# Two plain MLP groups instead of four, and five Strassen pairs instead of four, with each later Fourier mix set beside the next batch's attention

## The chip, the cores and the metric

The kernel runs on one core of one Trainium2 chip. The metric is the device time of one execution in microseconds (us). The core has five engines with a queue each: TensorE (PE in the profile, its weight loads PEld), VectorE (DVE), ScalarE (ACT), GpSimd (POOL) and SyncE (SP). Each works through its queue in order; semaphores make one wait for another. DMA transfers are issued from the queues of SP, ACT and POOL. Everything is float32, and each float32 matmul has two records in the trace (a transpose has one).

## The reference

```python
# attention: q, k, v (4, 8, 768, 64), lam (8,); blocks of 64 along the sequence
intra = (qb @ kb.T * Dmask) @ vb                  # Dmask[i, j] = lam ** (i - j) for i >= j
inter = (qb * lam_pow) @ kv_state
out = intra + inter
kv_state = lam_block * kv_state + (kb * rev_pow).T @ vb
x = out.transpose(0, 2, 1, 3).reshape(4, 768, 512)
# mix and MLP: w_ch1 (512, 2048), w_ch2 (2048, 512)
mixed = real(fft(fft(x, axis=1), axis=2))
u = x + mixed
un = (u - mean(u)) / sqrt(var(u) + 1e-6)          # over the last axis
return u + maximum(un @ w_ch1, 0) @ w_ch2
```

## The kernel before

**The front.** For each of the four batches, `attn(b)` computes the attention in six chunks of 128 rows, and `fft_ln(b)` the Fourier mix and the normalisation. One chunk: transposes of k and q (L314, L319), scores (L338, TensorE), scores times decay (L343, VectorE), the state (L358 on TensorE, L363 on VectorE), old state times q (L373), scores times v (L379), a turn back (L395), and copies by ACT. `kd`, the decayed k (L310), is made by POOL. x goes to DRAM, and POOL's queue gathers its mirrored rows (L489, L495 after chunk 4, L502 after the last chunk). The mix uses symmetry: VectorE folds x with its mirror (`fold_a`, `fold_b` or `folds_apart`, tiles `fe` and `fo`, L476 to L571), TensorE transforms along the sequence (L603, twenty products a batch), ACT copies to `ys`, TensorE transforms along the width (`width`, L615 to L620), and VectorE adds the result to x (`summed`, L691 to L704), three times. Then `stats` (L634, L635, with POOL's L638 and L639 for `rs`) and `norm` (L655) follow for three groups of 256 rows each, numbered 1, 2, 0.

**The MLP** of the twelve groups is done in two ways. A *plain* group is `mlp(b, g)`: `norm` transposes on TensorE (L660) and keeps `ut` in SBUF; the first layer is 64 products of 128x128x256 (L749), with the maximum on ACT (L757) or VectorE (L755), the second 32 products of 128x128x512 (L763). It can run beside the front. A *late* group goes to DRAM instead, transposed by VectorE (L668, four stores of 64 KB a tile on SP's queue), with its u (256 KB a tile). After the front, two late groups make a *pair*, done in Strassen's form: the first pair with one level in the first layer (L1031) and two in the second (L1198), the later, *deep* pairs with two levels in both (L1124 and L1198, 392 products of 128x128x128 each way). Two lines say which groups are which:

```python
    ORDER = [(b, g) for b in range(B) for g in (1, 2, 0)]
    PLAIN, LATE = ORDER[:4], ORDER[4:]
```

Strassen's form needs sums of weight quarters. `combine_weights(0)` and `(1)` (L837, sixteen VectorE operations, tiles `w1s`, `w2s` and, in place, the weights `w`) come after the front; their space is that of the front's tables. `front_sums` (L265) makes some more in the front and stores them by POOL's queue. `late()` then runs the pairs; the first pair starts with `begin`, six sets of products with plain weights, and the next product needs `w1s` and `sx` (L929, L931).

**The order.** What sets it is Python generators that yield an estimate of their time: `weave(lead, other, ratio)` takes steps of `other` whenever its sum lags behind that of `lead`, `beside` is a weave with a part of another generator, `chain` runs one after the other. Operations are emitted in that order, a scheduler may move them somewhat (`keep_in_program_order` and `high_priority` steer it), and then each engine's order is fixed. Before, the rest of the front is one chain, with each batch's attention and then its mix, and the plain groups lie along all of it:

```python
    fr = chain([att1, fft_ln(1)] + [front(b) for b in range(2, B)])
    run(beside(beside(chain(half[0]), t_half, w, 0.5 * NW), t_half + 0.5 * NW, fr, t_rest * t_half / t_back + 15.0))
    run(w)
    back = chain(half[1] + [mlp(*PLAIN[3])])
    run(weave(fr, back, (t_back - t_half) / (t_rest - t_rest * t_half / t_back)))
```

Three of the four plain groups are split into two halves of the hidden layer, since half of the weights arrive first (`w`, the generator that loads the weights and brings them to the form used, L226 to L235); what is left of the last plain group is emitted with `combine_weights(0)`. Batch 0's mix has run beside attention 1 already (`LEADS`), before the plain groups.

Of the kernel before, what the change touches and what calls it, by code (L numbers as in the profile page):

```python
# [77 lines left out]
def kernel(  # L78
# [11 lines left out]
    B, H, S, D = q.shape  # L90
# [38 lines left out]
    xp = plain_pool("xp", 2 * NC + 2)  # L129
    up = plain_pool("up", 3)  # L130
# [198 lines left out]
    def attn_out(b, c, head):  # L329
# [75 lines left out]
        if b not in TURNED:  # L405
# [9 lines left out]
            if (b, c) == (B - 1, 1):  # L415
                with tc.issue_after(grown.ins):
                    run(front_sums())
# [160 lines left out]
    def fft_ln(b):  # L578
# [7 lines left out]
        if b in LEADS:  # L586
            yield from fold_a(b)
            yield from fold_b(b, sets)
            yield 2.0
        else:  # L590
            yield 1.0
            run(fold_a(b))
            yield 6.0 if b - 1 in LEADS else 3.0
            run((folds_apart if b > 1 else fold_b)(b, sets))
            yield 27.0 if b - 1 in LEADS else 9.0
# [46 lines left out]
        def norm(g):  # L642
# [7 lines left out]
            for i in range(G):  # L650
                un = new(ep, [128, DM], "e") if i == 1 and (b, g) in (PLAIN[0], PLAIN[3]) else new(np_, [128, DM], "un", bufs=1)
                u = xs[b, TT[g][i]]
                with tc.high_priority(300) if (b, g) in PLAIN[1:3] else ExitStack():
                    for o, x in ((un[:, 0:HM], u[:, 0:HM]), (un[:, HM:DM], u[:, DM - 1:HM - 1:-1])):
                        nc.vector.tensor_scalar(o, x, mv[:, i, 0:1], rs[:, i:i + 1],  # L655
                                                op0=ALU.subtract, op1=ALU.mult)
# [63 lines left out]
        if b in LEADS:  # L720
            two, none = norm(2), norm(0)
            held.update({(b, 1, 1): two, (b, 1, 4): two, (b, 1, 7): none, (b, 1, FO): none})
            return
# [5 lines left out]
    PLAIN, LATE = ORDER[:4], ORDER[4:]  # L729
# [624 lines left out]
    def run(gen):  # L1354
        return sum(gen)
# [28 lines left out]
    half = [[mlp(b, g, h * FO // 2, (h + 1) * FO // 2) for b, g in PLAIN[:3]] for h in range(2)]  # L1384
    half[0][0] = mlp(*PLAIN[0], 0, FO // 2, half[0][1])
    fr = chain([att1, fft_ln(1)] + [front(b) for b in range(2, B)])
    t_rest, t_back = 3 * t_front - 5 * t_chunk, len(PLAIN) * t_mlp - 50.0
    t_half = 1.5 * t_mlp
    run(beside(beside(chain(half[0]), t_half, w, 0.5 * NW), t_half + 0.5 * NW, fr, t_rest * t_half / t_back + 15.0))
    run(w)  # L1390
    back = chain(half[1] + [mlp(*PLAIN[3])])
    run(weave(fr, back, (t_back - t_half) / (t_rest - t_rest * t_half / t_back)))
# [45 lines left out]
```

## Time and profile before

| | |
|---|---|
| three runs | 777.11, 777.5 and 780.93 us; median 777.5 us |
| span of the profiled execution | 771.7 us; its own time is not listed apart, 5.8 us lie between its span and the median |
| attention 0, mix 0 and most of attention 1 | 0 to 94.7 us |
| plain groups beside the front | from 94.7 us on |
| scores of batch 3's last chunk | 333.3 us |
| first product of the first Strassen pair | 409.6 us |
| first products of the three deep pairs | 501.4, 588.9 and 676.5 us |

The span is from the first to the last instruction on the core. A row of a table by stretches gives the length, then for each engine the busy time and in brackets its instructions, then the granted TensorE clock, the DMA share and the GB/s. A row of the timeline gives start, duration, engine, line, operation, tiles (out<-in), shape and count, and in brackets how long the engine had been idle and what ended that. Lines are those of the kernel before; in the changed kernel most of these stand three lines higher (L749 is L746 there).

### The profile page before, as it was taken

To read this page: it belongs to the slowest core of one execution; us is meant where nothing else is said; L and a number is where in the kernel's file an instruction comes from. 1 tells how busy PE (TensorE), PEld (TensorE's weight loads), DVE (VectorE), ACT (ScalarE), POOL (GpSimd) and SP (SyncE) were. 2 spreads that over 40 slices of the span, in tenths; PEclk is the share of its full clock that TensorE was granted. 3 is DMA by queue.
4 is the path that set the end of the run, shared out by engine and by line. 5 is a ranking of instruction groups with operands and counts; after the bars stand their busy time and mean duration, and the time that the engine had idled before them with its cause. 6 is when DMAs were issued, how large, how long until landed. Compare 5 with 4: busy or idle time off the path is not lost.

```text
span 771.7 us, 15006 instructions
## 1 busy us (share of the span) xinstructions
PE 752.6 (98%) x5784; PEld 646.7 (84%) x5784; DVE 602.8 (78%) x1167; ACT 231.1 (30%) x532; POOL 178.4 (23%) x202
## 2 busy tenths in 40 slices
PE   6989999999999999999999999999999999999997
PEld 5777877777685967769747899999999999999997
DVE  6999998784936575336898999788986699758984
ACT  3755443435521221322101221034301341024310
POOL 3223330021111113220105941360015001230013
PEclk9999999999999999999999999999999999999999
DMA  9979732347943149731433465876545456455442
GB/s 240 274 161 250 195 125 86 106 96 181 246 117 94 45 82 270 176 97 35 113 65 124 150 218 164 273 234 202 180 124 178 125 186 182 127 175 180 144 141 70
DMA packets 154924, 120.22 MB, mean 156 GB/s; under 512 B 114286, under 2 KB 116974, under 8 KB 154854
## 3 DMA queue, kind: packets, MB, share of 16 engines
q1 hardware_dynamic: 147792, 100.51, 46.7%
q0 software_dynamic: 4032, 12.99, 4.7%
q10 hardware_dynamic: 3030, 5.78, 2.1%
q8 instruction: 46, 0.75, 0.4%
q14 instruction: 24, 0.20, 0.1%
HBM read 88.04 MB, written 31.20 MB: 155 GB/s over the span
## 4 chain that ended last, share of the span: by engine, by line
PE 88%; DVE 7%; DMA 2%; ACT 1%; issue 1%; POOL 0%; SPq 0%; DVEq 0%; ACTq 0%
PE p L1198 22%; PE p L1124 17%; PE pm L763 13%; PE pm L749 13%; PE p L1031 6%; PE pa L603 3%; PE pa L379 3%; PE pa L338 3%; PE pa L373 2%; PE pa L314 1%; PE pa L358 1%; PE pa L395 1%; DVE sc L343 1%; PE pa L763 1%; PE pa L319 1%
## 5 line engine op out<-in xcount | busy, mean ns | idle before, releaser
L749 PE MATMUL pm<-ut,w 128*128 128x256 f32 x512 | 118.3, 381 | 0.0
L763 PE MATMUL pm<-w,hr 128*128 128x512 f32 x240 | 108.7, 596 | 0.1
L749 PEld LDWEIGHTS pm<-ut,w 128*128 128x128 f32 x512 | 94.7, 190 | 14.4 <-issue 2.7
L763 PEld LDWEIGHTS pm<-w,hr 128*128 128x128 f32 x240 | 43.8, 190 | 45.5 <-issue 43.8
L1219 POOL TENSOR_TENSOR y<-y,u 128x512 f32<-128x512 f32 x12 | 19.9, 1661 | 186.8 <-DVE y L1228 155.5
L1198 PE MATMUL p<-tx,sx 128*128 128x128 f32 x400 | 52.7, 275 | 0.0
L1198 PEld LDWEIGHTS p<-tx,sx 128*128 128x128 f32 x400 | 48.6, 192 | 0.0
L1133 DVE TENSOR_TENSOR ha<-p,ha 128x512 f32<-128x512 f32 x60 | 40.1, 686 | 8.6 <-PE p L1124 8.6
L1204 ACT COPY y<-p 128x128 f32<-128x128 f32 x48 | 12.8, 266 | 103.6 <-PE p L1198 103.1
L310 POOL TENSOR_TENSOR kd<-k,decay 128x512 f32<-128x512 f32 x20 | 21.7, 1083 | 86.5 <-PE pa L358 50.1
L343 DVE TENSOR_TENSOR sc<-pa,decay 128x512 f32<-128x512 f32 x48 | 30.9, 683 | 11.7 <-PE pa L338 11.5
L1206 DVE TENSOR_TENSOR y<-p,y 128x128 f32<-128x128 f32 x92 | 25.6, 285 | 15.6 <-PE p L1198 9.1
L1198 PE MATMUL p<-w,ha 128*128 128x128 f32 x288 | 37.4, 275 | 0.0
L1133 DVE TENSOR_TENSOR hs<-p,hs 128x512 f32<-128x512 f32 x39 | 26.2, 685 | 12.4 <-PE p L1124 12.4
L338 PEld LDWEIGHTS pa<-qT,kT 64*128 64x128 f32 x384 | 25.1, 193 | 12.2 <-ACT qT L321 6.4
L1198 PEld LDWEIGHTS p<-w,ha 128*128 128x128 f32 x288 | 34.9, 192 | 0.1
L638 POOL TENSOR_SCALAR ve<-mv 128x2 f32<-128x2 f32 x12 | 6.2, 519 | 120.0 <-DVE mv L635 120.0
L757 ACT ACTIVATE hr<-pm 128x256 f32<-128x256 f32 x44 | 16.7, 382 | 57.6 <-PE pm L749 53.7
L1124 PE MATMUL p<-sx,tx 128*128 128x128 f32 x264 | 33.9, 275 | 0.0
L338 PE MATMUL pa<-qT,kT 64*128 64x128 f32 x384 | 30.1, 292 | 2.9 <-ACT qT L321 2.9
L1124 PEld LDWEIGHTS p<-sx,tx 128*128 128x128 f32 x264 | 31.7, 192 | 0.0
L379 PE MATMUL pa<-sc,v 128*64 128x128 f32 x384 | 28.9, 282 | 1.3 <-DVE sc L343 1.0
(274 smaller groups left out, 1748.4 us busy)
## 6 DMA issues: line engine op xcount, KB each, us to landing
tx<-td SPq DMA_DIRECT2D x84, 256.0 KB, 2.9
raw<-in_moe_w_ch_dram SPq DMA_DIRECT2D x32, 512.0 KB, 4.3
tx<-sd SPq DMA_DIRECT2D x63, 256.0 KB, 2.8
k<-in_k_dram SPq DMA_DIRECT2D x24, 256.0 KB, 3.7
q<-in_q_dram SPq DMA_DIRECT2D x24, 256.0 KB, 7.0
v<-in_v_dram SPq DMA_DIRECT2D x24, 256.0 KB, 5.7
td<-tx SPq DMA_DIRECT2D x21, 256.0 KB, 2.0
ud<-x SPq DMA_DIRECT2D x16, 256.0 KB, 3.1
```

The lines of the kernel that those rows point to most:

```text
L310: nc.gpsimd.tensor_tensor(kd, kt, kpow, op=ALU.mult)
L338: mm(pss[hi][:, hp, :], lhsT=kT[HD[hi], hp, :], rhs=qT[HD[hi], hp, :], start=True, stop=True)
L343: nc.vector.tensor_tensor(t, pss[hi], decay[:, hi::2, :], op=ALU.mult)
L379: mm(po[HD[hi], hp, :], lhsT=vt[:, 2 * hp + hi, :], rhs=sc[hi][:, hp, :], start=(c == 0 and hp == 0), stop=(hp == HP - 1), skip_group_chec ...
L603: mm = nc.tensor.matmul(ps[:, n, :], lhsT=piece(a, i, n), rhs=cs[0:rows, a, i in (2, 3), n, :], start=(a == 0), stop=(a == 1))
L749: nc.tensor.matmul(ps, lhsT=w1[:, c, 128 * fc:128 * fc + 128], rhs=ut[:, c, :], start=(c == 0), stop=(c == KO - 1))
L763: return nc.tensor.matmul(ps, lhsT=hr[(fc - f0) // 4][:, fc % 4, 128 * i:128 * i + 128], rhs=w2[:, fc, :], start=(fc == f0), stop=(fc == f ...
L1031: nc.tensor.matmul(ps, lhsT=s2.A[a][:, kt, 128 * i:128 * i + 128], rhs=U[b][:, kt, :], start=(first and kt == 0), stop=(kt == 1), skip_gro ...
L1124: nc.tensor.matmul(ps[:, 128 * i:128 * i + 128], lhsT=ab[m][0][:, 128 * i:128 * i + 128], rhs=ab[m][1], start=(start and i == 0), stop=Tru ...
L1133: V.tensor_tensor(o, p, o, op=ADD)
L1198: nc.tensor.matmul(ps[:, 0:HM // 2], lhsT=ab[m][0][i], rhs=ab[m][1][:, i, :], start=(start and i == 0), stop=(i == HF // 2 - 1), skip_grou ...
L1206: V.tensor_tensor(o, ps[:, 0:HM // 2], o, op=ADD)
```

## The change

Two groups (the first two, both of batch 0) stay plain, and ten become late: five pairs, four of them deep. Both plain groups are split into halves. The first halves run beside the weights, attention 1's rest, mix 1 woven with 0.8 of attention 2, and attention 2's rest. Then mix 2 is woven with 0.4 of attention 3, `front_sums` follows mix 2 instead of attention 3's second chunk, then comes attention 3's rest, and 0.35 of a plain group's time is given to all this and 0.35 to mix 3; what is then left of them is emitted with `combine_weights(0)`. Group (0, 0) and group (1, 1) now take the late way through `norm`. Pools: four more x tiles, one less `ut`.

```diff
--- before.py
+++ after.py
@@ -126,8 +126,8 @@
     fp = front_pool("fp", 1)
     np_ = front_pool("np", 2)
     ep = front_pool("ep", 2)
-    xp = plain_pool("xp", 2 * NC + 2)
-    up = plain_pool("up", 3)
+    xp = plain_pool("xp", 2 * NC + 4)
+    up = plain_pool("up", 2)
     hp_ = plain_pool("hp", FO // 4)
     dram = ctx.enter_context(tc.tile_pool(name="dram", bufs=1, space=bass.MemoryType.DRAM))
     PS = bass.MemoryType.PSUM
@@ -412,9 +412,6 @@
                 nc.scalar.dma_start(xd[b][0][(c - 1) * C:c * C], x)
             if c >= NC - 2:
                 nc.scalar.dma_start(xd[b][1][(c - NC + 2) * C:(c - NC + 3) * C], x)
-            if (b, c) == (B - 1, 1):
-                with tc.issue_after(grown.ins):
-                    run(front_sums())
             if c == NC - 2 and b - 1 not in LEADS:
                 mirror_a(b)
             elif last:
@@ -590,9 +587,9 @@
         else:
             yield 1.0
             run(fold_a(b))
-            yield 6.0 if b - 1 in LEADS else 3.0
+            yield 3.0
             run((folds_apart if b > 1 else fold_b)(b, sets))
-            yield 27.0 if b - 1 in LEADS else 9.0
+            yield 9.0
 
 
         for i in (0, 1, 4, 2, 3):
@@ -648,9 +645,9 @@
 
                 to = utd[b, g] = dram.tile([128, KO, G * 128], F32, name=f"utd{b}{g}")
             for i in range(G):
-                un = new(ep, [128, DM], "e") if i == 1 and (b, g) in (PLAIN[0], PLAIN[3]) else new(np_, [128, DM], "un", bufs=1)
+                un = new(ep, [128, DM], "e") if i == 1 and (b, g) == PLAIN[0] else new(np_, [128, DM], "un", bufs=1)
                 u = xs[b, TT[g][i]]
-                with tc.high_priority(300) if (b, g) in PLAIN[1:3] else ExitStack():
+                with tc.high_priority(300) if (b, g) == PLAIN[1] else ExitStack():
                     for o, x in ((un[:, 0:HM], u[:, 0:HM]), (un[:, HM:DM], u[:, DM - 1:HM - 1:-1])):
                         nc.vector.tensor_scalar(o, x, mv[:, i, 0:1], rs[:, i:i + 1],
                                                 op0=ALU.subtract, op1=ALU.mult)
@@ -719,14 +716,14 @@
             stats(after)
         if b in LEADS:
             two, none = norm(2), norm(0)
-            held.update({(b, 1, 1): two, (b, 1, 4): two, (b, 1, 7): none, (b, 1, FO): none})
+            held.update({(b, 1, 1): two, (b, 1, 4): two, (b, 1, 6): none, (b, 1, 7): none, (b, 1, FO): none})
             return
         yield 1.0
         yield from norm(0)
 
 
     ORDER = [(b, g) for b in range(B) for g in (1, 2, 0)]
-    PLAIN, LATE = ORDER[:4], ORDER[4:]
+    PLAIN, LATE = ORDER[:2], ORDER[2:]
 
     out_low, out_high = dram_disjoint_views(out.rearrange("b s d -> (b s) d"), 2)
 
@@ -1381,15 +1378,19 @@
     run(beside(part(mix, T_FOLD), T_FOLD, att1, 3.25 * t_chunk))
     run(beside(mix, 24.0, beside(att1, 2.75 * t_chunk, w, 0.16 * NW), 0.16 * NW + 1.75 * t_chunk))
 
-    half = [[mlp(b, g, h * FO // 2, (h + 1) * FO // 2) for b, g in PLAIN[:3]] for h in range(2)]
+    half = [[mlp(b, g, h * FO // 2, (h + 1) * FO // 2) for b, g in PLAIN] for h in range(2)]
     half[0][0] = mlp(*PLAIN[0], 0, FO // 2, half[0][1])
-    fr = chain([att1, fft_ln(1)] + [front(b) for b in range(2, B)])
-    t_rest, t_back = 3 * t_front - 5 * t_chunk, len(PLAIN) * t_mlp - 50.0
-    t_half = 1.5 * t_mlp
-    run(beside(beside(chain(half[0]), t_half, w, 0.5 * NW), t_half + 0.5 * NW, fr, t_rest * t_half / t_back + 15.0))
+    t_mix, t_att = 33.0, NC * t_chunk
+    att2, att3, mix2 = attn(2), attn(3), fft_ln(2)
+    t_one = t_mix + t_att
+    one = chain([att1, beside(fft_ln(1), t_mix, att2, 0.8 * t_att), att2])
+    run(beside(chain(half[0]), t_mlp, beside(w, 0.6 * NW, one, t_one), 0.6 * NW + t_one))
     run(w)
-    back = chain(half[1] + [mlp(*PLAIN[3])])
-    run(weave(fr, back, (t_back - t_half) / (t_rest - t_rest * t_half / t_back)))
+    run(one)
+    back = chain(half[1])
+    two = chain([beside(mix2, t_mix, att3, 0.4 * t_att), mix2, front_sums(), att3])
+    run(beside(two, t_one, back, 0.35 * t_mlp))
+    run(beside(fft_ln(3), t_mix, back, 0.35 * t_mlp))
     front_end.close()
     s2.wp = ctx.enter_context(tc.tile_pool(name="ws", bufs=1, side="left", reuse_waits="tile"))
     s2.up = ctx.enter_context(tc.tile_pool(name="us", bufs=1, side="left", reuse_waits="tile"))
```

Where this puts the work on the engines is seen at three places. First, TensorE at batch 2's mix: the end of its products along the sequence (`cs`, L603 before and L600 now) and the first along the width (`dt`). Before:

```order
L603 MATMUL pa_2644<-cs,fo_2478 128x193
L749 MATMUL pm_2650<-ut_1409,w_129 128x256 x4
L615 MATMUL pa_2656<-dt,ys_134 128x128
L616 MATMUL pa_2656<-dt,ys_132 128x129
L617 MATMUL pa_2656<-dt,ys_136 128x129
L618 MATMUL pa_2656<-dt,ys_133 128x128
L620 MATMUL pa_2656<-dt,ys_135 128x128
L749 MATMUL pm_2681<-ut_1409,w_129 128x256 x4
L615 MATMUL pa_2687<-dt,ys_134 128x128
```

and now:

```order
L600 MATMUL pa_2625<-cs,fo_2382 128x193
L612 MATMUL pa_2631<-dt,ys_134 128x128
L613 MATMUL pa_2631<-dt,ys_132 128x129
L614 MATMUL pa_2631<-dt,ys_136 128x129
L615 MATMUL pa_2631<-dt,ys_133 128x128
L617 MATMUL pa_2631<-dt,ys_135 128x128
L358 MATMUL pa_2645<-v_2542,kd_2546 64x64 x8
L373 MATMUL pa_2656<-qs_2562,sd 64x128 x8
L379 MATMUL pa_2656<-sc_2611,v_2542 64x128
```

Between the mix's products stood products of a plain group (`w`, `ut`); now attention 3's chunk 1 follows them (state L358, old state L373, scores times v L379).

Second, TensorE from the last products of batch 3's mix along the width to the first pair's first product (L1031 before, L1028 now). Before, where `pm` is the plain groups' PSUM tile:

```order
L749 MATMUL pm_3687<-ut_1732,w_129 128x256 x4
L749 MATMUL pm_3727<-ut_1732,w_129 128x256 x4
L749 MATMUL pm_3752<-ut_1732,w_129 128x256 x4
L763 MATMUL pm_3781<-w_130,hr_3460 128x512 x4
L763 MATMUL pm_3781<-w_130,hr_3511 128x512 x4
L763 MATMUL pm_3781<-w_130,hr_3566 128x512 x4
L763 MATMUL pm_3781<-w_130,hr_3678 128x512 x4
L763 MATMUL pm_3808<-w_130,hr_3460 128x512 x4
L763 MATMUL pm_3808<-w_130,hr_3511 128x512 x4
L763 MATMUL pm_3808<-w_130,hr_3566 128x512 x4
L763 MATMUL pm_3808<-w_130,hr_3678 128x512 x4
L1031 MATMUL p_3864<-ur_3775,w_129 128x256 x2
```

and now:

```order
L612 MATMUL pa_3406<-dt,ys_134 128x128
L613 MATMUL pa_3406<-dt,ys_132 128x129
L614 MATMUL pa_3406<-dt,ys_136 128x129
L615 MATMUL pa_3406<-dt,ys_133 128x128
L617 MATMUL pa_3406<-dt,ys_135 128x128
L613 MATMUL pa_3420<-dt,ys_132 128x129
L614 MATMUL pa_3420<-dt,ys_136 128x129
L615 MATMUL pa_3420<-dt,ys_133 128x128
L1028 MATMUL p_3582<-ur_3509,w_129 128x256 x2
L1028 MATMUL p_3583<-ur_3509,w_129 128x256 x2
```

The three rows of a plain group's first layer and its 32 products of the second layer are no longer there: the first pair's products follow the mix's last ones directly. Ahead of batch 3's mix (`L600`) now stand eight products of a plain group.

Third, VectorE at the start of the weight combining (`w1s`, L837 before and L834 now), behind the last statistics of batch 3 (`stt`, `mv`). Before:

```order
L635 BN_AGGR mv_3716<-stt_3717 128x2
L634 BN_STATS stt_3720<-x_3435 128x6
L655 TENSOR_SCALAR un_3703<-x_3386,mv_3648,rs_3656 128x256 x2
L635 BN_AGGR mv_3716<-stt_3720 128x2
L755 TENSOR_SCALAR hr_3678<-pm_3752 128x256
L837 TENSOR_TENSOR w1s<-w_129 128x1024 x2
L837 TENSOR_TENSOR w1s<-w1s,w_129 128x1024
L668 STREAM_TRANSPOSE e_3706<-un_3703 128x512
L837 TENSOR_TENSOR w1s<-w1s,w_129 128x1024
L655 TENSOR_SCALAR un_3734<-x_2940,mv_3716,rs_3724 128x256 x2
L837 TENSOR_TENSOR w1s<-w_129,w1s 128x1024 x2
```

and now:

```order
L701 TENSOR_TENSOR x_3214<-pa_3420,xn_3069 1x128
L631 BN_STATS stt_3457<-x_2564 128x6
L631 BN_STATS stt_3460<-x_3214 128x6
L632 BN_AGGR mv_3456<-stt_3457 128x2
L632 BN_AGGR mv_3456<-stt_3460 128x2
L834 TENSOR_TENSOR w1s<-w_129 128x1024
L665 STREAM_TRANSPOSE e_3431<-un_3428 128x512
L834 TENSOR_TENSOR w1s<-w_129 128x1024
L652 TENSOR_SCALAR un_3443<-x_3162,mv_3395,rs_3403 128x256 x2
L834 TENSOR_TENSOR w1s<-w1s,w_129 128x1024 x2
L834 TENSOR_TENSOR w1s<-w_129,w1s 128x1024
L665 STREAM_TRANSPOSE e_3446<-un_3443 128x512
```

The combining stands at the same place behind the statistics, between the norms (`un`) and transposes (`e`) of the last groups; the maxima of the plain group (`hr`, L755) are gone.

## The prediction

> **What bounds the kernel now.** I read the page first (busy shares and the forty slices), then a table of five stages, then the rows of the last mix and of what follows it.
>
> ```profile
> PE 752.6 (98%) x5784; PEld 646.7 (84%) x5784; DVE 602.8 (78%) x1167; ACT 231.1 (30%) x532; POOL 178.4 (23%) x202
> PE   6989999999999999999999999999999999999997
> ```
>
> TensorE (PE) is busy 98% of the span and has no thin slice between the first and the last. The next table gives, for each stretch, its length and then busy time with instruction counts for PE, PEld, VectorE (DVE), ACT and POOL, then the granted clock and the DMA share.
>
> ```profile
> 0.00:94.70 94.70, 82.22 (x948) 69.35 (x949) 84.68 (x172) 53.48 (x122) 29.09 (x38) 1.00 0.90 221
> 94.70:333.30 238.60, 238.60 (x1539) 175.89 (x1537) 160.66 (x358) 83.32 (x193) 43.56 (x57) 1.00 0.49 135
> 333.30:409.70 76.40, 76.00 (x336) 52.76 (x336) 55.64 (x108) 8.85 (x27) 9.20 (x12) 1.00 0.33 88
> 409.70:501.30 91.60, 90.24 (x593) 83.33 (x592) 83.09 (x143) 16.25 (x48) 48.38 (x41) 1.00 0.55 186
> 501.30:771.70 270.40, 265.56 (x2379) 265.37 (x2377) 218.72 (x390) 69.15 (x144) 48.23 (x55) 1.00 0.52 160
> ```
>
> The five stretches are: attention 0 and mix 0 without plain groups; the plain groups beside the rest of the front; the last mix and the weight combining (the "tail", counted from the scores of batch 3's last chunk); the first Strassen pair; the three deep pairs. From 94.7 on TensorE never waits, so a stage costs what TensorE has in it, as long as it has something. In the tail VectorE is busy 55.64 of 76.40 us with a chain of its own, and TensorE is full only because plain groups stand there.
>
> **What is added: one deep pair.** First L1124, then L1198, each over the first two deep pairs:
>
> ```profile
> 501.30:588.85 87.55, 44.91 (x392) 44.34 (x393) 1.00 0.57 179
> 588.85:676.40 87.55, 44.92 (x392) 44.34 (x393) 1.00 0.53 163
> ```
>
> ```profile
> 501.30:588.85 87.55, 44.92 (x395) 44.34 (x393) 1.00 0.57 179
> 588.85:676.40 87.55, 44.92 (x395) 44.34 (x393) 1.00 0.53 163
> ```
>
> Two deep pairs follow each other at 87.55 us, with all their loads, VectorE sums and stores inside (DMA share 0.57). A fourth adds **87.55**.
>
> **What is removed.** Two plain groups: 64 products L749, 35 L763 before the last chunk's scores and the rest behind them (counts from the order: 192 and 89 products precede those scores now, 128 and 54 afterwards; a product is two records). Records of both, in stretches where they run alone:
>
> ```profile
> 343.64 10.36 PE pm L749 x48
> 382.00 27.73 PE pm L763 x64
> ```
>
> So 0.216 and 0.433 us a record. Ahead of the last scores go 128 x 0.216 + 70 x 0.433 = 58.0 us, and 16 transposes of u, 1.7 us by L660's 3.44 us for 24 records:
>
> ```profile
> 94.70:333.30 238.60, 3.44 (x24) 2.90 (x24) 1.00 0.49 135
> ```
>
> That is **-59.6**, and since TensorE is full from 94.7 to 333.3, it is time of the end, if nothing else becomes late: 238.6 us shrink to 179.0.
>
> **What is late next, in the middle.** VectorE's 160.7 us of that stretch stay: four maxima go, and groups (0,0) and (1,1), now late, take four 32x32 transposes, 0.7 us each by the ten of L668 there:
>
> ```profile
> 94.70:333.30 238.60, 6.97 (x10) 1.00 0.49 135
> ```
>
> Their 16 stores of transposed u and 4 of u join SP's queue, in a stretch with a DMA share of 0.49 that would become about 0.65; the first stage ran with 0.90. VectorE must then be busy 90% of 179 us. I cost those stores, the pool sizes, the moved weight sums (12 sums on VectorE and 12 stores on POOL's queue; behind those stand kd of chunk 2 and rs of mix 2, each needed only after sums that stand earlier on VectorE) and the later `held` norms at nothing by themselves, but their cover is VectorE's slack, and that is what runs out. The nearest row is the end of the first stage, mix 0 beside attention 1:
>
> ```profile
> 60.00:94.70 34.70, 32.23 (x364) 28.48 (x365) 32.73 (x70) 18.89 (x46) 10.86 (x10) 1.00 0.85 228
> ```
>
> TensorE gets 32.23 of 34.70, 93%; 179.0 / 0.93 = 192.7, so 13.7 us lost. I take **+15**, since mix 2 now has only attention matmuls around it (the second place of the order). Ends: 0 (plain matmuls fill every gap, as now) and +36 (the 60 us ahead of that row: 82.22 - 32.23 = 50.0 busy, 83%; 179.0 / 0.83 = 215).
>
> **The tail.** From the last chunk's scores to the first product that needs combined weights (start, us, what, idle before it and its end):
>
> ```profile
> 333.27 1.16 PE L338 MATMUL pa<-qT,kT 64*128 64x128 f32 x16
> 334.36 2.84 PE L763 MATMUL pm<-w,hr 128*128 128x512 f32 x6
> 341.77 0.33 ACTq L414 DMA_DIRECT2D xb<-xn  x1
> 344.56 1.29 POOL L502 DMA_INDIRECT x<-xb,ix  x1 [4.76 <-DMA xb<-xn]
> 348.33 0.68 DVE L516 TENSOR_TENSOR fe<-x,x 128x512 f32<-128x512 f32 x1
> 348.94 0.41 DVE L755 TENSOR_SCALAR hr<-pm 128x256 f32<-128x256 f32 x1
> 349.27 0.41 DVE L517 TENSOR_TENSOR fe<-fe 128x255 f32<-128x255 f32 x1
> 358.96 0.42 DVE L542 TENSOR_TENSOR fo<-fo 65x256 f32<-65x256 f32 x1
> 367.43 0.42 DVE L691 TENSOR_TENSOR ds<-pa,bs 128x256 f32<-128x256 f32 x1 [5.58 <-ACT ds L687]
> 386.69 2.36 DVE L837 TENSOR_TENSOR w1s<-w 128x1024 f32<-128x1024 f32 x2 [0.82 <-POOL rs L639]
> 407.46 1.22 DVE L837 TENSOR_TENSOR w<-w 128x1024 f32<-128x1024 f32 x1
> 410.59 0.42 DVE L797 TENSOR_TENSOR y<-pm,x 128x256 f32<-128x256 f32 x1 [1.91 <-DMA out_dram<-y]
> 411.98 0.69 DVE L931 TENSOR_TENSOR sx<-ur,sx 128x512 f32<-128x512 f32 x1
> 415.02 1.03 PE L1031 MATMUL p<-sx,w1s 128*128 128x256 f32 x4
> ```
>
> That is one chain on VectorE: folds, three sums with norms, weight combining (386.7 to 408.7), inputs; 81.7 us from 333.3 to 415.0. TensorE spent 27.7 of them in the quoted L763 run and 10.4 in the L749 run. In the new order eight L763 products and two more stand behind the last scores (20 x 0.433 = 8.7 us), then the 40 records of L603 (7.1 us, below), 18 small products L615 to L620, and 24 records of L1031 that need no combined weights (5.2): some 25 us of work in a chain of 70. What the chain itself sheds: 1.7 before the gather (three L763 products stand between scores and state, one afterwards), so the second folds start 13 us after the scores; eight L755 maxima (0.33 each by the starts 348.94 and 349.27: 2.7); one pair of y additions (0.7); the wait for a y store (1.9); and 2.3 of the 8.1 between 359.4 and 367.4, because the 16 records of L603 on fo no longer stand behind plain products. The waits for POOL's rs stay. In all 9.3; the inputs stand right behind the weights, and L1031's wait for its turn (412.7 to 415.0) goes too, 2.3: **-12** (11.6), a tail of about 70. Ends: nothing shed, 0; no wait left on VectorE behind the gather, -20.3: its busy 50.4 us (below) less 3.4 for maxima and additions, 13 ahead and 1.4 for the inputs make 61.4.
>
> ```profile
> 333.30:409.70 76.40, 7.05 (x40) 6.73 (x40) 1.00 0.33 88
> 348.30:411.30 63.00, 62.85 (x255) 44.05 (x253) 50.37 (x99) 7.60 (x24) 3.12 (x7) 1.00 0.31 79
> ```
>
> The first row is L603 alone, the second all engines. VectorE at 50.4 of 63.0 us is the reason that TensorE's saving doesn't come through here.
>
> **TensorE after a pause.** Now it never pauses mid-kernel. At the start it does, and the same work is slower (scores and state of chunks 0 and 1):
>
> ```profile
> 7.96 2.08 PE L338 MATMUL pa<-qT,kT 64*128 64x128 f32 x16 [0.68 <-ACT qT L321]
> 9.97 1.12 PE L358 MATMUL pa<-v,kd 128*64 128x64 f32 x16
> 15.91 1.16 PE L338 MATMUL pa<-qT,kT 64*128 64x128 f32 x16 [0.46 <-ACT qT L321]
> 17.00 0.69 PE L358 MATMUL pa<-v,kd 128*64 128x64 f32 x16
> ```
>
> 1.35 us lost over 32 records. The tail gets about three pauses of several us (folds, then the way to L615, then the combining). One of them stands on the path: **+1.5**, ends 0 and 4 (three). The Trainium skill, page "TensorE: Matmul & The Clock Gate", section "Why this matters for your kernels", says that an idle stretch over some 3 us puts the matmul clock back to half; its Part 1 gives 3.4 us until it is full again. The start agrees with it; no run here shows it later. By the rule each pause costs at most an estimated 1.7 us, three of them 5, and the sum would be 813.5 in place of 810.
>
> **Sum**, against the profiled execution, of which the page gives the span: 87.55 - 59.6 + 15 - 12 + 1.5 = +32.4. Its span of 771.7 becomes 804.1. Around the span I leave what stands there now (777.5 of the median less 771.7, 5.8 us): 809.9, so **810**.
>
> **Rivals.**
> - *The middle stays full.* Then its 15 us fall to between 0 and 7, and a tail near its short end makes +8 to +22: 785 to 800. For it: 160.7 of 179 us of VectorE is not yet all. Against it: the row 60.00:94.70, where VectorE at 94% went with TensorE at 93%.
> - *VectorE bounds the middle.* Mix 2, attention 3 and the weight sums take turns on one engine, with waits for ACT and POOL between; 30 to 36 us are lost there, or the tail sheds nothing: +44 to +68, 822 to 845. For it: 83% in the first 60 us. Against it: those include the start at 5 us and a DMA share of 0.90.
> - *Not slower.* One mechanism, in the tail: VectorE's chain runs through with no wait at all, the folds not even waiting for the gather, since all else has drained. Then 3 us of scores, 4 of first folds, 47.0 and 1.4 make 55.4 instead of 81.7, -26.3; with a full middle the sum is +1.7, 779. It decides only if the tail falls under 53.8 us with nothing lost ahead. For it: nothing but VectorE's busy share there; against it: 4.76 and 5.58 us of waits that follow from data. If even the tail were filled by TensorE, the two groups (256 x 0.216 + 128 x 0.433 + 1.7 = 112.4) less 87.55 would give 25 us back, 753; the order leaves no plain product there to do it.
>
> **Chances and range.** Forecast 0.50 (800 to 822), full middle 0.20, VectorE-bound middle 0.24, not slower 0.06. From 790 to 834 I leave out about half of the first rival's span, the last one, and the top of the second, under 2 in 10. Half a per cent, 3.9 us, is about what a measurement of this kernel can tell from no change: faster than 773.6 is 0.02, within 0.04, slower 0.94.
>
> **What would show it.** Right: four deep pairs of 87.5 us each; the last scores near 289 us; TensorE with its thin slices right behind them, some 45 us idle until L1028 is steady, each wait ended by VectorE; TensorE at 90 to 95% from 94.7 to there. Wrong: plain products found late beside the combining; a tail under 60 us; deep pairs that take another time; or q, k, v loads that come late on SP's queue behind the new stores, which I cost at nothing.

## The result, and the profile after

The changed kernel takes 821.73 us (median of four runs, 819.45 to 824.09) against 777.31 for the kernel before on the same chip: 1.057 times the time, 95% interval 1.0536 to 1.0603. Its profiled execution took 821.29 us with a span of 819.5, 47.8 us more than the span of before. The medians differ by less, 44.4 us: each listed run takes about 2 us more than its span, so the profiled execution of before, with its 771.7, took an estimated 774 us, less than any of the four runs behind the median (776.9 to 780.9).

From the page of the changed kernel, the busy time of each engine and two rows of the forty slices, TensorE and its granted clock:

```profile
PE 744.7 (91%) x6168; PEld 669.9 (82%) x6168; DVE 667.3 (81%) x1273; ACT 244.3 (30%) x556; POOL 194.4 (24%) x216
PE   6889999999498997527999999999999999999997
PEclk9999999999799997768999999999999999999999
```

TensorE is busy for less time than before (744.7 against 752.6 us), and where the row of before had 9 in every slice but the first, the third and the last there are now two holes: one near 205 to 225 us (the 4), one from 310 to 375 us (7, 5, 2, 7). In both the granted clock falls too. The next table is the changed kernel by stage, with the columns of the table of before; the stages end at the last chunk's scores, at the first product with combined weights, and then with each pair.

```profile
0.00:94.70 94.70, 79.39 (x921) 66.52 (x922) 82.69 (x167) 51.67 (x114) 26.19 (x36) 0.98 0.85 213
94.70:301.33 206.63, 189.12 (x1351) 142.72 (x1349) 160.50 (x350) 78.21 (x183) 48.56 (x56) 0.98 0.64 165
301.33:373.90 72.57, 36.08 (x172) 27.87 (x173) 55.22 (x106) 6.97 (x22) 10.31 (x13) 0.74 0.35 90
373.90:461.60 87.70, 87.00 (x568) 79.91 (x569) 78.98 (x138) 15.16 (x45) 47.30 (x40) 0.98 0.58 195
461.60:549.15 87.55, 87.55 (x787) 87.55 (x786) 78.19 (x140) 23.08 (x48) 20.59 (x23) 1.00 0.59 179
549.15:636.70 87.55, 87.55 (x787) 87.55 (x786) 71.25 (x127) 23.08 (x48) 13.72 (x16) 1.00 0.54 163
636.70:724.25 87.55, 87.55 (x786) 87.55 (x786) 71.26 (x127) 23.09 (x48) 13.69 (x16) 1.00 0.55 164
```

The deep pairs are as long as before, and there is one more. The middle is 206.6 us instead of 238.6, though the plain work taken out of it was 59.6. The tail, with most of its plain work gone, is 72.6 us instead of 81.7: VectorE is busy 55.2 us of it and TensorE 36.1.

**The first hole.** The timeline of the changed kernel from 191 us on; the columns are start, length, engine, line and what it works on. On SP the length is that of a run of issues.

```profile
191.10 22.46 SPq L669 DMA_DIRECT2D utd<-e  x16
...
208.29 0.72 ACT L228 ACTIVATE e<-e,cvt 128x512 uint16<-128x512 uint16 x1 [4.22 <-DVE e L226]
...
209.34 6.27 PE L746 MATMUL pm<-ut,w 128*128 128x256 f32 x20 [5.01 <-ACT hr L754]
...
210.24 0.71 DVE L665 STREAM_TRANSPOSE e<-un 128x512 f32<-128x512 f32 x1
...
213.66 1.04 SPq L214 DMA_DIRECT2D raw<-in_moe_w_ch_dram  x2
...
215.74 0.91 SPq L303 DMA_DIRECT2D k<-in_k_dram  x1
...
218.16 0.43 DVE L226 TENSOR_SCALAR e<-raw 128x512 uint16<-128x512 uint16 x1 [4.95 <-DMA raw<-in_moe_w_ch_dram]
...
222.72 1.11 PE L314 MATMUL pa<-ident,k 128*128 128x128 f32 x4 [7.11 <-DMA k<-in_k_dram]
```

SP's queue stands for 22 us in sixteen stores of transposed u, four for each of four transposes of VectorE, the last of which starts at 210.2. Behind them stand raw weights and k. k is issued at 215.7 and TensorE, whose order has k's transposes next, waits for it until 222.7; VectorE waits 4.95 us for the raw weights behind the same stores. The hole has another part that is not the queue's: the 5.0 us in which TensorE is idle ahead of 209.3 end with a maximum on ScalarE, which stood behind a weight conversion (L228) that waited 4.22 us for VectorE.

**The second hole.** TensorE in the changed kernel's tail, from the last chunk's scores on:

```profile
301.26 1.16 PE L338 MATMUL pa<-qT,kT 64*128 64x128 f32 x16
...
306.86 7.03 PE L760 MATMUL pm<-w,hr 128*128 128x512 f32 x16
319.57 8.52 PE L600 MATMUL pa<-cs,fe 128*128 128x193 f32 x24 [5.68 <-DVE fe L523]
327.88 3.40 PE L600 MATMUL pa<-cs,fo 128*128 128x193 f32 x16
...
344.58 7.89 PE L1028 MATMUL p<-ur,w 128*128 128x256 f32 x24 [9.29 <-DMA ur<-utd]
373.90 2.04 PE L1028 MATMUL p<-sx,w1s 128*128 128x256 f32 x4 [21.43 <-DVE sx L928]
```

Three waits, 5.7 us for the folds, 9.3 for the load of transposed u and 21.4 for the combining and the inputs on VectorE.

### The profile page after: what moved, and what is told of

The parts are those of the page before. It is cut to its first block, busy times and chain, and to the rows that moved or that the text cites. A ratio compares the mean times of both kernels' runs of the same rounds, so it can differ in the third digit from the quotient of the medians.

```text
span 819.5 us, 16108 instructions
## 1 busy us (share of the span) xinstructions
PE 744.7 (91%) x6168; PEld 669.9 (82%) x6168; DVE 667.3 (81%) x1273; ACT 244.3 (30%) x556; POOL 194.4 (24%) x216
## 4 chain that ended last, share of the span: by engine, by line
PE 70%; DVE 15%; DMA 6%; issue 4%; SPq 2%; POOL 1%; ACT 1%; DVEq 0%; POOLq 0%; ACTq 0%
PE p L1195 24%; PE p L1121 21%; PE pm L760 5%; PE pm L746 4%; PE p L1028 4%; PE pa L600 3%; PE pa L338 2%; PE pa L379 2%; DMA k<-in_k_dram 2%; PE pa L373 1%; DVE un L652 1%; SPq L303 1%; DVE sc L343 1%; PE pa L760 1%; DVE stt L631 1%
## 5 line engine op out<-in xcount | busy, mean ns | idle before, releaser
L1216 POOL TENSOR_TENSOR y<-y,u 128x512 f32<-128x512 f32 x15 | 25.1, 1675 | 251.4 <-DVE y L1225 155.5
L746 PE MATMUL pm<-ut,w 128*128 128x256 f32 x256 | 63.6, 398 | 5.0 <-ACT hr L754 5.0
L1130 DVE TENSOR_TENSOR ha<-p,ha 128x512 f32<-128x512 f32 x80 | 53.5, 685 | 11.5 <-PE p L1121 11.3
L746 PEld LDWEIGHTS pm<-ut,w 128*128 128x128 f32 x256 | 48.8, 198 | 14.1 <-ACT hr L754 5.4
L760 PE MATMUL pm<-w,hr 128*128 128x512 f32 x112 | 52.3, 601 | 0.0
L1195 PE MATMUL p<-w,ha 128*128 128x128 f32 x360 | 46.7, 275 | 0.0
L1128 ACT COPY ha<-p 128x512 f32<-128x512 f32 x32 | 18.7, 584 | 64.0 <-PE p L1121 62.8
L1121 PE MATMUL p<-ur,w 128*128 128x128 f32 x288 | 37.4, 275 | 0.0
L1028 PE MATMUL p<-sx,w1s 128*128 128x256 f32 x64 | 17.1, 397 | 21.4 <-DVE sx L928 21.4
L760 PEld LDWEIGHTS pm<-w,hr 128*128 128x128 f32 x112 | 19.9, 190 | 18.8 <-issue 18.4
L1121 PEld LDWEIGHTS p<-ur,w 128*128 128x128 f32 x288 | 34.7, 192 | 0.0
L1028 PE MATMUL p<-ur,w 128*128 128x256 f32 x96 | 26.1, 418 | 9.3 <-DMA ur<-utd 9.3
```

Of the source, the lines that this page charges most:

```text
L746: nc.tensor.matmul(ps, lhsT=w1[:, c, 128 * fc:128 * fc + 128], rhs=ut[:, c, :], start=(c == 0), stop=(c == KO - 1))
L760: return nc.tensor.matmul(ps, lhsT=hr[(fc - f0) // 4][:, fc % 4, 128 * i:128 * i + 128], rhs=w2[:, fc, :], start=(fc == f0), stop=(fc == f ...
L1028: nc.tensor.matmul(ps, lhsT=s2.A[a][:, kt, 128 * i:128 * i + 128], rhs=U[b][:, kt, :], start=(first and kt == 0), stop=(kt == 1), skip_gro ...
L1121: nc.tensor.matmul(ps[:, 128 * i:128 * i + 128], lhsT=ab[m][0][:, 128 * i:128 * i + 128], rhs=ab[m][1], start=(start and i == 0), stop=Tru ...
L1128: nc.scalar.copy(o, p)
L1130: V.tensor_tensor(o, p, o, op=ADD)
```

## The experiments

The question is which of the two holes costs what, and what would fill them. The theory: the middle waits for loads on SP's queue, the tail is VectorE's chain, and two plain groups are too little for both. The rivals: the middle is VectorE's own chain (so that the loads only happen to be last), or the order and not the number of groups loses the time. The table has the landmarks of every run in its profiled execution: start of the last chunk's scores, of the first product with combined weights, of the first deep pair; the tail is the second less the first.

| run | median, us | to before (95%) | last scores | tail | first deep pair |
|---|---|---|---|---|---|
| before | 777.3 | 1 | 333.3 | 81.7 | 501.4 |
| after | 821.7 | 1.054 to 1.060 | 301.3 | 72.6 | 461.7 |
| e1, loads on ACT | 798.5 | 1.021 to 1.029 | 270.5 | 83.4 | 439.6 |
| e2, more plain work in the tail | 822.4 | 1.052 to 1.059 | 296.6 | 81.3 | 462.8 |
| e7, both | 807.8 | 1.035 to 1.043 | 273.0 | 89.5 | 449.0 |
| e3, four groups | 788.1 | 1.009 to 1.016 | 328.1 | 98.6 | 512.9 |
| e12, four groups, loads on ACT | 786.3 | 1.009 to 1.014 | 329.2 | 100.4 | 516.1 |
| e4, two groups, old order | 838.0 | 1.071 to 1.083 | 321.1 | 70.1 | 478.6 |
| e5, w2s on POOL | 826.5 | 1.063 to 1.067 | 301.6 | 77.6 | 466.9 |
| e6, idle products | 850.1 | 1.093 to 1.100 | 299.6 | 104.8 | 489.7 |
| e8, e1 and e5 | 808.8 | 1.041 to 1.046 | 270.7 | 91.2 | 447.8 |
| e9, sums postponed | 826.5 | 1.061 to 1.066 | 300.9 | 63.6 | 466.2 |
| e10, e1 and e9 | 809.0 | 1.039 to 1.044 | 268.5 | 79.9 | 446.1 |
| e11, e10 with maxima on ACT | 813.0 | 1.044 to 1.050 | 275.2 | 80.4 | 454.1 |

**The loads on another queue (e1).**

```diff
-            nc.sync.dma_start(t, src[b, :, rows, :].rearrange("h p d -> p h d"))
+            (nc.scalar if b > 1 else nc.sync).dma_start(t, src[b, :, rows, :].rearrange("h p d -> p h d"))
```

> The q, k, v loads of batches 2 and 3 are issued on ScalarE's queue instead of SP's, where they stood behind the 16 stores of transposed u. Theory A (the hole of TensorE near 205 to 223 us is made by those stores, which keep SP's queue from issuing k): the hole shrinks from about 18 us of idle time to a few, the last scores come 8 to 14 us earlier, and the plain products that the new order lets stand behind the scores add a little: 805 to 813 us. Theory B (the hole is the chain of the second gather, the folds and the transposes on VectorE, and the loads only happen to be last): at most 3 us come back, 818 us or more. Theory C (loads on ScalarE's queue hold up its copies): slower than 822.

It takes 798.53 us, 23.2 less than the changed kernel, more than theory A's 8 to 14 for the loads and something for the plain work. With this edit alone the scheduler placed 64 records of L746 and 46 of L760 behind the last scores, instead of 20 of L760: 64 x 0.216 + 26 x 0.433 = 25.1 us of plain work went from the middle to the tail. So e1 alone doesn't tell the loads from the moved work; e2 and e7 do.

**Plain work held back, without and with the loads (e2, e7).** The plain products of the second halves are pinned in place (the first of each accumulation keeps the program's order), and fewer steps of `back` are taken beside `two`; e7 adds the edit of e1.

```diff
-    run(beside(two, t_one, back, 0.35 * t_mlp))
-    run(beside(fft_ln(3), t_mix, back, 0.35 * t_mlp))
+    run(beside(two, t_one, back, 0.15 * t_mlp))
+    pinned.append(True)
+    run(beside(fft_ln(3), t_mix, back, 0.5 * t_mlp))
```

> Some 38 us of the plain groups' second halves are held back until after the scores of batch 3's last chunk, so that they stand in the tail; nothing else is changed. Theory A (the tail is a chain of VectorE with about 36 us in which TensorE has nothing, and the middle is as long as TensorE's work plus its holes): the tail grows by under 10 us, the middle shrinks by 25 to 35: 795 to 805 us. Theory B (the middle is as long as the front's own chain, so that TensorE only idles more there): within 5 us of 822. Theory C (the products in the tail delay the last mix's own matmuls by as much as they cost): 822 or more.

> The kernel with the plain products held back into the tail (822.4 us), and the q, k, v loads of batches 2 and 3 on ScalarE's queue besides. Theory A (that kernel gained nothing because its front was held by late loads, 14 us for q and 8 for k, and not by TensorE): both waits go, the last scores come 20 to 30 us earlier, 790 to 802 us. Theory B (the front is a chain on VectorE with or without the loads): 810 us or more.

In e2, 88 records of L746's line and 64 of L760's stand behind the last scores, 46.7 us by 0.216 and 0.433, 38.1 more than in the changed kernel. The middle became only 4.7 us shorter and the tail 8.7 longer: no change (822.4). That is theory B's time, but the waits say why. TensorE in e2's middle and tail, by what it waits for (total, times, longest):

```profile
PE pa L319 <- DMA q<-in_q_dram: 14.0, 1, 14.0
PE p L1035 <- DVE y L802: 9.4, 1, 9.4
PE pa L314 <- DMA k<-in_k_dram: 8.0, 1, 8.0
```

Then the same two stretches (to the last scores, and to the first product with combined weights) in e2, in e7 and in e1:

```profile
98.20:296.60 198.40, 156.17 (x1192) 121.27 (x1191) 154.86 (x338) 73.89 (x171) 46.14 (x54) 0.91 0.65 166
296.60:377.90 81.30, 69.02 (x304) 48.33 (x305) 61.59 (x118) 9.27 (x29) 11.63 (x16) 0.94 0.34 89
```

```profile
95.50:273.00 177.50, 156.59 (x1190) 123.08 (x1188) 149.07 (x334) 73.98 (x170) 40.85 (x51) 0.89 0.66 172
273.00:362.50 89.50, 73.78 (x304) 51.42 (x305) 64.06 (x122) 9.32 (x29) 13.43 (x19) 0.89 0.38 105
```

```profile
97.90:270.50 172.60, 160.03 (x1232) 121.02 (x1230) 151.11 (x338) 75.33 (x173) 41.86 (x51) 0.99 0.68 179
```

With the same plain work in the same place (156.2 and 156.6 us of TensorE), the loads' queue decides 23.6 us of the last scores, 20.9 of them in the middle itself (198.4 less 177.5 us): both long waits are gone in e7, as theory A had it. That came at 807.8, between both theories' times, because the tail gave 8.2 us back. From the last scores to the mix's first product it takes 21.9 us instead of 17.4: VectorE's first folds of the last mix wait for the store of a weight sum that `front_sums` keeps in their buffer. In e2 that sum was stored at 279.6 us, 17 us ahead of the last scores; in e7 VectorE makes it at 276.9, after the last scores, and its store goes out at 281.1, behind three gathers on POOL's queue. From VectorE's waits in e7's tail:

```profile
DVE fe L473 <- DMA sd<-fe: 6.7, 1, 6.7
```

Then TensorE starts the mix after a pause. The 56 records from there to L612 in e7 and, the same 56, in e2:

```profile
295.00:313.00 18.00, 17.92 (x56) 12.50 (x57) 7.82 (x21) 2.03 (x4) 0.00 (x0) 0.75 0.04 15
```

```profile
314.00:328.50 14.50, 13.76 (x56) 9.62 (x57) 7.92 (x21) 2.04 (x4) 0.03 (x1) 1.00 0.05 18
```

At a granted clock of 0.75 instead of 1.00 they take 3.5 us longer. With the 4.5 us ahead that is the 8.2; from L612 on both tails last 49.4 us.

In e1 VectorE is busy 151 of 172.6 us, 88%, and TensorE 93%, near the row that the prediction went by. But the loads are not the whole of what the middle loses. In the five runs with two plain groups and these loads on ScalarE's queue the last scores come at 268.5 to 275.2 us, and they come no earlier in e7, which holds 13.0 us more plain work back, than in e1; TensorE is idle 20.9 us of e7's middle and 12.6 of e1's. So the front then has a length of its own, 173.8 to 180.5 us from 94.7 on. Which chain sets it is not shown.

**Number of groups and order (e3, e4, e12).** e3 has the new order with four plain groups (three of them in halves, the fourth whole), four late pairs and the pools of before; e4 has two plain groups in the old order; e12 is e3 with the loads on ACT.

```diff
-    PLAIN, LATE = ORDER[:2], ORDER[2:]
+    PLAIN, LATE = ORDER[:4], ORDER[4:]
...
-    run(beside(two, t_one, back, 0.35 * t_mlp))
-    run(beside(fft_ln(3), t_mix, back, 0.35 * t_mlp))
+    run(beside(two, t_one, back, 1.2 * t_mlp))
+    run(beside(fft_ln(3), t_mix, back, 0.6 * t_mlp))
```

```diff
-    one = chain([att1, beside(fft_ln(1), t_mix, att2, 0.8 * t_att), att2])
...
+    fr = chain([att1, fft_ln(1)] + [front(b) for b in range(2, B)])
+    t_rest, t_back = 3 * t_front - 5 * t_chunk, len(PLAIN) * t_mlp - 25.0
...
+    run(weave(fr, back, (t_back - t_half) / (t_rest - t_rest * t_half / t_back)))
```

> The new order of the front, but four plain groups and four late pairs as before, with the pools as before. Theory A (the time is lost because two groups are too little work for the front): TensorE is full again and the time is that of before within 8 us, 772 to 785. Theory B (the new order itself makes the late loads and the hole): 790 us or more, with a hole of 10 us or more in TensorE between 200 and 330 us.

> Two plain groups and five late pairs as in the changed kernel, but each batch's attention and mix one after the other, with the weight sums in attention 3, as before. Theory A (the number of plain groups decides): a middle with holes and a tail of about 70 us again, 812 to 835 us. Theory B (the order decides): 800 us or less.

> Four plain groups in the new order (788.1 us) with the loads of batches 2 and 3 on ScalarE's queue. Theory A (what that order loses with four groups is the late loads too): 775 to 782 us. Theory B (its tail of 98.6 us is full of TensorE's work, so an earlier front only moves plain work): 786 to 790.

e3 fits neither theory: 788.1, three us above theory A's range and below theory B's. TensorE is nearly full again, as the stages of e3 show:

```profile
95.60:328.10 232.50, 225.51 (x1479) 166.65 (x1477) 157.22 (x353) 81.03 (x189) 48.54 (x56) 0.99 0.51 137
328.10:426.70 98.60, 97.57 (x417) 68.20 (x417) 62.27 (x122) 11.43 (x35) 10.60 (x15) 1.00 0.27 74
```

So the number of groups is what empties TensorE, and it is worth 33.6 us between e3 and the changed kernel. The new order by itself costs 10 us with four groups (TensorE is idle 7.0 us of that middle) and saves 16 with two: e4 takes 838.0, 16.2 more than the changed kernel and a little above theory A's range. In e4 no plain product at all is left behind the last scores. In e12 the earlier loads change nothing (786.3): its tail is full of TensorE's work (99.35 of 100.4 us busy), as theory B has it.

**The tail: sums on POOL (e5, e8), sums postponed (e9, e10).** e5 gives the six sums `w2s` to POOL; e8 does so on top of e1.

```diff
-                V.tensor_tensor(o[:, i:i + n // 2], x[:, i:i + n // 2], y[:, i:i + n // 2], op=op)
+                late = part == 0 and any(o is z for z in later)
+                (nc.gpsimd if late else V).tensor_tensor(o[:, i:i + n // 2], ..., op=op)
```

> The changed kernel, with the six sums w2s of the weight combining on GpSimd instead of VectorE; the first products don't need them. Theory A (the tail is one chain on VectorE and every us taken from it comes back): six sums of about 1.2 us go, -6 to -8: 814 to 816 us. Theory B (GpSimd and VectorE slow each other, or another wait, such as that for rs or for the transposed u, is as late): 819 us or more.

> The loads of batches 2 and 3 on ScalarE's queue (798.5 us alone) and the six sums w2s on GpSimd. Theory A (both are on the path, one in the middle and one in the tail, and they add up): 790 to 793 us. Theory B (with more plain work in the tail the combining is no longer what ends it): 796 us or more.

Both are slower, in theory B's ranges: 826.5, 4.8 more than the changed kernel, and 808.8, 10.2 more than e1. VectorE in e5 while POOL makes its sums, and POOL's:

```profile
349.41 3.37 DVE L836 TENSOR_TENSOR w1s<-w 128x1024 f32<-128x1024 f32 x1 [1.13 <-POOL rs L636]
...
355.98 4.77 DVE L652 TENSOR_SCALAR un<-x,mv,rs 128x256 f32<-128x256 f32 x2
360.68 6.63 DVE L836 TENSOR_TENSOR w1s<-w1s,w 128x1024 f32<-128x1024 f32 x2
367.23 1.21 DVE L836 TENSOR_TENSOR w1s<-w,w1s 128x1024 f32<-128x1024 f32 x1
```

```profile
349.34 5.63 POOL L836 TENSOR_TENSOR w2s<-w 128x1024 f32<-128x1024 f32 x2
354.94 11.29 POOL L836 TENSOR_TENSOR w2s<-w,w2s 128x1024 f32<-128x1024 f32 x4
```

As long as POOL works, to 366.2, VectorE's sums take more than twice as long (6.63 for two that take 2.36 in the changed kernel), and the two TENSOR_SCALAR of `un`, with one tile as input, 4.77 instead of 0.73; its transpose (0.70) is no slower. At 367.2 a sum is back to 1.21. This is theory B's first reason. The Trainium skill, page "SBUF — State Buffer", section "Who interferes with whom", says that a VectorE instruction with two inputs in SBUF and a GpSimd instruction that reads SBUF contend for a shared port and the later one waits for the other; the rows of the sums agree.

e9 leaves POOL alone and takes eight sums (`w2s`, `b12`) behind the inputs on VectorE, two beside each of four blocks of the first layer; e10 does it on top of e1.

```diff
+        rest = combine_weights(2)
...
+                run(part(rest, 2.0))
                 keep_sums(i)
```

> The changed kernel; eight of the fourteen sums of the weight combining (w2s and b12, which the first layer doesn't read) stand behind the inputs sx on VectorE, two beside each of the first four blocks of the first layer. Theory A (the tail is VectorE's chain; only GpSimd's work beside it spoiled the run with w2s there): 8 x 1.2 = 9.6 us come off the tail and the first pair has the slack for them: 811 to 815 us. Theory B (VectorE's slack in the first pair, 79.0 busy of 87.7, is too small): the tail gives 9.6 and the pair takes it back, 818 to 823. Theory C (the tail waits for something else, so that sx is no earlier): 819 or more and the same tail.

> Loads of batches 2 and 3 on ScalarE's queue, and the eight sums postponed. Theory A (middle and tail are separate terms that add): 798.5 less the gain of the postponed sums alone, 787 to 792 us. Theory B (with plain products in the tail, their y additions and stores end it): 795 or more.

The tail of e9 is 63.6 us, 9.0 less than the changed kernel's: nearly all of the 9.6 us of VectorE's sums come off it, so the tail is VectorE's chain. But the first pair now takes 101.7 us from its first product with combined weights to the first deep pair, against 87.8, and the whole is 4.8 longer. Theory B has the right mechanism and too small a size: 13.9 us are lost for 9.6 moved; TensorE is busy 91.7 of the 101.7 us and waits five times for VectorE's `ha`, 9.6 us in all. Two of e9's postponed sums, and POOL's sums for the second layer beside them:

```profile
377.29 4.49 DVE L839 TENSOR_TENSOR w<-w 128x1024 f32<-128x1024 f32 x2
```

```profile
378.45 2.25 POOL L859 TENSOR_TENSOR w<-w 128x512 f32<-128x512 f32 x1
```

The pair takes 4.49 us where it takes 2.33 in the changed kernel's tail, and POOL's operation 2.25 where those of its line take 1.26 to 1.45 there. In e10 the tail sheds only 3.5 us against e1, and the first pair takes 97.7 us instead of 85.7 (809.0 in all): theory B's range, without a test of its reason.

**Maxima on ScalarE (e11).**

```diff
-            if fc % 2 and f1 == FO:
+            if False:
                 nc.vector.tensor_scalar(t, ps, 0.0, None, op0=ALU.max)
```

> As the run before (loads on ScalarE's queue, sums postponed), and the 16 maxima of the plain groups' second halves on ScalarE instead of VectorE. Theory A (with the loads out of the way the front is VectorE's chain, 151 us busy of 173): some 5 us of VectorE's work go, 2 to 5 us shorter than without. Theory B (the wait for PSUM banks of the plain products, now on an engine with its own queue of loads, gets longer): no shorter, or longer.

813.0 against 809.0, half a per cent: the last scores come 6.6 us later than in e10. That is theory B's sign, but the waits of TensorE for these maxima (8.6 us in e10) are gone, and a wait of 8.8 us for VectorE's folds of batch 2's mix is there instead. So theory B's reason is not seen in these waits, and the cause stays open.

**Idle products in the pauses (e6).**

```diff
             ps = psum_a([128, 2, NK])
+            for _ in range(32 if b == B - 1 and i == 0 else 0):
+                tc.keep_in_program_order(nc.tensor.matmul(ps[:, 0, :], lhsT=w1[:, 0, 0:128], rhs=w1[:, 0, 128:128 + NK], ...))
...
+            for _ in range(96 if j == 0 and i == 0 else 0):
+                tc.keep_in_program_order(nc.tensor.matmul(Z, lhsT=w1[:, 0, 0:128], rhs=w1[:, 0, 128:384], ...))
```

> The changed kernel, with products whose results are overwritten unread in two pauses of TensorE in the tail: 32 ahead of L600 of the last mix, 96 ahead of the first product with combined weights. Theory A (after a pause TensorE runs at half its pace for about 10 us of work, as 12.8 us for the 40 records of L600 against 7.1 show): L600 takes 7.1 to 7.5 us and the whole is 5 to 8 us shorter, 814 to 817. Theory B (the pace comes back within some 3 us, the rest of L600's time is waiting for its inputs): 1 to 3 us shorter, 819 to 821. Theory C (the chain on VectorE hides it): 821 to 823.

The whole time tells nothing of the theories (850.1 us): 96 products are 192 records, and these took 41.6 us where the pause had 21.4. The first 32 tell something. TensorE in e6:

```profile
305.21 10.62 PE L598 MATMUL pa<-w 128*128 128x193 f32 x64
317.75 0.59 PE L602 MATMUL pa<-cs,fe 128*128 128x193 f32 x2 [1.92 <-DVE fe L523]
319.09 5.55 PE L602 MATMUL pa<-cs,fe 65*128 65x193 f32 x22 [0.75 <-DVE fe L523]
```

The 24 records on fe are 6.1 us busy instead of 8.5, with a pause of 1.9 us ahead of them instead of 5.7; the 40 records of L600 take 9.1 us, more than theory A's 7.1 to 7.5, since the granted clock over those 24 is still only 0.75. What this would bring to the whole stays open; e7 against e2 has the price of such a pause, 3.5 us.

## Why the prediction was right

The forecast of slower by about 32 us came out as 44, for the reasons given in the main, with one term too small. Some of the nearness is luck. Span against span it is 47.8, where the forecast had 32.4; of the 5.8 us that it added around the span some 2 stand around any span here, and the rest comes from the short profiled execution of before. 821.7 also lies at the very edge between its 800 to 822 and the 822 to 845 of the rival "VectorE bounds the middle". By its own steps, against the span:

| term | forecast | measured |
|---|---|---|
| a fourth deep pair | +87.55 | +87.5 (357.8 us from the first deep pair to the end, 270.3 before) |
| plain work out of the middle | -59.6 | -59.6, but see the next line |
| TensorE lost in the middle | +15 (0 to +36) | +27.6: 206.6 us less 179.0 |
| the tail, with slow pace after pauses | -12 + 1.5 | -9.1 |
| first pair | 0 | +1.4 |
| sum | +32.4 | +47.8 |

**The middle is the term that was mis-sized.** The prediction took the 93% of the end of the first stage, where VectorE was nearly full. Here VectorE was busy 160.5 of 206.6 us, 78%, with 4.95 us of waiting for late weights inside, so a full VectorE was not the bound. The step that failed is the one that costed the moved stores on SP's queue at nothing, and named as what would show it wrong "q, k, v loads that come late on SP's queue behind the new stores". The loads were late: TensorE waited 7.1 us for k in the changed kernel. In e2, where less plain work covers such waits, that queue costs 23.6 us of the last scores, by comparison with e7. It is not all of the loss: counted as in the table, e1, with its loads moved, still loses 21.9 us in the middle (270.5 - 94.7 = 175.8, less 179.0 - 25.1), where the changed kernel loses 27.6. So the rival "VectorE bounds the middle" is not ruled out for what is left, and what the loads alone cost, with the plain work in its place, stays open. Windows of TensorE in the changed kernel around it (length, busy, records, clock, DMA share, GB/s):

```profile
195.00:205.00 10.00, 8.45 (x68) 1.00 0.66 163
205.00:215.00 10.00, 5.66 (x18) 0.83 0.59 115
215.00:225.00 10.00, 2.89 (x11) 0.74 1.07 258
225.00:235.00 10.00, 10.00 (x88) 0.91 0.79 159
```

Of the 27.6 us, 13.0 are idle in these 40 us, 4.4 in two other places (105 to 125 and 245 to 265 us, 2.2 each), 2.9 came before the first plain product (97.7 us instead of 94.8), and the rest is time in which TensorE was busy at a lower clock, as in these rows, or is not explained here. That VectorE itself waited 4.95 us for raw weights behind the same stores was in no term either.

**The tail** was right in kind and near in size: VectorE's chain, as e9 shows, of 72.6 us where about 70 were forecast, with TensorE idle for 36.5 us where 45 were. The savings lie elsewhere than forecast, though: 2.3 us from the scores to the mix's first product, 0.2 in the mix's L600, where 2.3 were expected, and 6.7 from there on. What the missing plain products left free in L600 went into the slow pace. So the nearness of this term is partly luck. Of the three waits that the prediction expected VectorE to end, the one of 9.3 us was ended by a load.

**The pace after a pause** was costed at 1.5 us. TensorE in the changed kernel's tail, around its three pauses; the number behind the count of records is the granted clock:

```profile
306.80:314.00 7.20, 7.09 (x19) 1.00 0.54 148
319.50:324.00 4.50, 4.34 (x12) 0.50 0.18 62
324.00:328.00 4.00, 4.00 (x14) 0.50 0.00 0
328.00:331.00 3.00, 3.00 (x17) 0.82 0.00 0
344.50:349.00 4.50, 4.42 (x11) 0.50 0.76 167
373.90:377.00 3.10, 3.10 (x8) 0.52 0.42 155
377.00:380.00 3.00, 3.00 (x16) 1.00 0.25 90
```

At half clock the 24 records of L600 on fe took 8.52 us where 24 x 0.176 = 4.2 is their time alone, and the 16 on fo 3.40 instead of 2.8. From 319.6 to the next products at 331.1 the 40 records needed 11.5 us, 4.5 more than the 7.05 of before, above the forecast's upper end of 4 for all three pauses. In the 3.1 us from 373.9 on TensorE got through 8 records, 8 x 0.216 = 1.7 us of work: another 1.4. The rule of the Trainium skill that the prediction weighed (page "TensorE: Matmul & The Clock Gate", section "Why this matters for your kernels", with Part 1) is borne out in kind: each pause over 5 us in the tail is followed by a clock of 0.50 to 0.52. The return to full clock took about 3 us after the last pause, as the page has it, but over 8 after the first. At the kernel's start, where the prediction saw the rule agree, only the pace does: the clock recorded there is 1.00 from 0 to 18 us.

**The rivals.** "The middle stays full" needed TensorE at 179 us there; it was 206.6. "Not slower" needed a tail under 53.8 us; even with eight of the sums taken out (e9) it is 63.6.

**No variant here beats the kernel before.** The nearest with five pairs is e1, 1.021 to 1.029 times its time: the fourth deep pair's 87.55 us are paid in full, and no run here wins back more than e1's 23 us. Whether an order that fills both holes would beat it was not tried.

## What to carry to other kernels

When work that filled an engine is taken away, look at what the queues then hold in order: here stores that waited for VectorE held up every load issued behind them on the same queue, and a load that had slack became late. Moving work from a chain onto engines or into a stage that are busy next need not help: here the sums given to GpSimd made the tail longer, and those postponed came back, with more, in the first pair. Cost the pace after a pause from rows of a kernel that has such a pause, where there is one, and not from the start of the kernel.

## What the hardware showed that was not expected

- VectorE and GpSimd working on SBUF at the same time slow each other: two sums of 128x1024 took 6.63 us on VectorE beside GpSimd's, 2.36 without (e5); 4.49 against 2.33 in e9, where GpSimd's 128x512 sum took 2.25 against 1.26 to 1.45.
- After a pause of 5.7 us TensorE's granted clock stayed at 0.50 for at least 8.5 us; after one of 21.4 us it was full again after about 3.
